# New places for the buffers of a convolution's backward pass, and two reordered steps, in a training kernel of four layers

## The chip, the cores and the metric

The kernel runs on one core of a Trainium2 chip. The metric is the time of one execution on the device, in microseconds (us). The trace is one execution recorded by the hardware profiler. Its engines are PE (TensorE, matrix products into PSUM), ACT (ScalarE), DVE (VectorE), POOL (GpSimd) and SP (SyncE, which here only issues transfers). Each engine takes its own instructions in the order in which the program was laid out, and waits for the others through semaphores.

## The reference

The program is the forward and the backward pass of four residual layers on a sequence of 2048 positions and 512 channels: convolution layer A, MLP layer B, A again, B again, with shared weights.

```python
def _A_ref(q, k, v, shift_k, ssm_k, ssm_D):          # convolution layer
    k_shift = sum over t of 4 taps: k_pad[:, t:t+S, :] * shift_k[:, ks-1-t]
    kv = k_shift * v
    y = irfft(rfft(kv padded to 2S) * rfft(ssm_k padded to 2S))[:S]
    y = y + kv * ssm_D
    return q * y

def _B_ref(x, w1, b1, w2, b2):                       # MLP, hidden width 1376
    h = gelu(einsum("bsd,df->bsf", x, w1) + b1)
    return einsum("bsf,fd->bsd", h, w2) + b2

x = A_q
x = x + _A_ref(layernorm(x), A_k, A_v, A_shift_k, A_ssm_k, A_ssm_D)
x = x + _B_ref(layernorm(x), B_w1, B_b1, B_w2, B_b2)
x = x + _A_ref(layernorm(x), ...)                    # same weights again
x = x + _B_ref(layernorm(x), ...)
# outputs: x, and by jax.vjp the gradients of q, k, v, shift_k, ssm_k, ssm_D, w1, b1, w2, b2
```

The kernel does the transforms as products with sine and cosine tables. The convolution `y` is computed once, since it doesn't depend on `x`.

## The kernel before: the parts that matter here

The run has these stages: tables and convolution forward (0 to about 210 us), MLP forward (to about 460), MLP backward (to about 640), then the backward pass of the convolution. Beside this last stage a second stream of work runs, the gradients of the MLP weights (`weight_grads`): the convolution's code yields after each step a number of microseconds, and that much of `weight_grads` is put in behind it. PE and DVE keep this program order.

**The start.** `sin_of` fills a table: phases on POOL for the first 1024 columns and on DVE for the rest, a bit mask on DVE, the sine on ACT. The constants of the fifth, five-row table `sp5` (for one tap row of the filter) are made before the first table.

```python
def sin_of(nc, consts, pool, out, krow, pv, shift, np_=P):
    for c0 in range(0, n, 1024):
        u = pool.tile([P, 1024], I32, name="tab_u", tag="tab_u", bufs=3)[0:np_, 0:w]
        eng = nc.gpsimd if c0 == 0 else nc.vector
        eng.tensor_scalar(out=u, in0=krow[...], scalar1=pv, scalar2=float(shift), ...)     # L182
    for c0, w, u in reversed(us):
        nc.vector.tensor_single_scalar(out=u, in_=u, scalar=8191, op=ALU.bitwise_and)
        nc.scalar.activation(out=out[...], in_=u, func=ACT.Sin, ...)
# phase_conv_forward
    pvh = iota_f32(...); pvn = iota_f32(...)
    pi5 = gp.tile([5, 1], I32, name="pi5")
    nc.vector.memset(pi5, 0)
    nc.gpsimd.iota(pi5[0:4, :], ...)                      # L467
    pv5 = gp.tile([5, 1], F32, name="pv5")
    nc.vector.tensor_copy(out=pv5, in_=pi5)
    ...                                                   # (cut)
    for cc in range(ND):                                  # four tables, each followed by
        sin_of(nc, consts, gp, tabN[...], krow, pvn[...], ...)
        h_chunk(cc)                                       # transposes of the filter: PE, then DVE casts hA, hsp
```

**MLP forward.** `o_ps` sums the residual and eleven products of the hidden layer in one PSUM bank.

```python
    for t in range(TS):                                   # b_fwd, TS = 4
        ps = m.psum.tile([P, D], F32, name="o_ps", tag="oo", bufs=4)
        nc.tensor.matmul(ps, lhsT=m.ident, rhs=x[:, t, :], start=True, stop=False)         # L1097
        for c in range(NFC):                              # NFC = 11
            nc.tensor.matmul(ps, lhsT=h[:, c, ...], rhs=w.w2[:, c, :], start=False, stop=(c == NFC - 1))   # L1099
        nc.scalar.activation(out=x[:, t, :], in_=ps, func=ACT.Identity)
```

**Convolution backward.** All pools here lie on the right side of SBUF; a pool that closes gives its room to the next one opened, and a new tile waits for the last use of the tiles under it (`reuse_waits="tile"`).

```python
    with tc.tile_pool(name="cb_w", side="right", ...) as wp:
        W = [wp.tile([P, 2, 8, 512], BF16, name=f"Wb{m}") for m in range(2)]
        ...                                                      # (cut) spectra, inverse blocks (DVE) into W[.][.., 4:8]
        with tc.tile_pool(name="cb_io", side="right", ...) as io:
            wdiag = io.tile([P, ND, 4, P], BF16, name="wdiag_b")
            ksbs = [io.tile([P, 4, D], BF16, name="ksb_b", tag="ksb", bufs=4) for i in range(4)]
            ...
            gT = io.tile([P, ND, S + 16], BF16, name="gksT")
            for i in range(4):
                for h in range(4):
                    gkv = W[h % 2][:, h // 2, 4 + i, :]
                    ...                                          # DVE products, PE transposes gt_ps
                    if h >= 2:
                        pr = psum.tile([P, 2, 512], F32, name="gr_ps", tag="sp", bufs=2)
                        ...                                      # 4 PE transposes
                        for cc in range(ND):                     # 4 evictions into W[1]
                            nc.scalar.activation(out=W[1][:, cc // 2, ...], in_=pr[:, 0, ...], func=ACT.Identity)   # L794
                    nc.scalar.activation(out=gT[...], in_=ps[...], func=ACT.Identity)                 # L797
                yield 3.0
                ...                                              # stores of ksb, unflip_rows
            kcs = [gyp.tile([P, 4096], BF16, name="kTc", tag="Sg", bufs=2)[:, 0:4 * 544] for cc in range(2)]
            kcs += [w0f[:, 2048 + 2176 * x:2048 + 2176 * (x + 1)] for x in range(2)]   # w0f: W[0], flat
            for cc in range(ND):
                dma(out=kcs[cc], in_=dram.kT[:, cc, :, :])       # dma = nc.gpsimd.dma_start, L809
            ...                                                  # gradient of k: 256 products gk_ps, 16 evictions, 4 stores
            gwo = io.tile([P, 2, ND, 4], F32, name="gwo", tag="gwo", bufs=1)
            junk = W[0][:, 0, 0:2, :]
            for cc in range(ND):                                 # gradient of the four taps
                for j in range(4):
                    for half in range(2):                        # g_ from gT, or from W[1]
                        nc.vector.scalar_tensor_tensor(out=junk, in0=g_, in1=kc[...], accum_out=gwo[...], ...)
                    yield 2.2
    with tc.tile_pool(name="cb_gh", side="right", ...) as hp:    # gradient of the long filter
        tabG = hp.tile([P, 2, 16, NQP], BF16, name="tabG")       # NQP = 272
        ...                                                      # 2 loads of tabG
        w0 = hp.tile([P, 2, 8, NQP], BF16, name="Wh", tag="Wh", bufs=2)
        th0 = [hp.tile([P, 2, 2, NQP], BF16, name=f"ibh{x}", tag=f"ibh{x}", bufs=3) for x in range(3)]
        gh0 = hp.tile([P, S], BF16, name="gh", tag="gh", bufs=4)
        for cc in range(ND):
            ...                      # 57 products gh_ps (PE) in 8 PSUM tiles, 11 evictions into Wh (ACT, L871 and L875)
            yield 7.0
            ...                      # inverse blocks of Wh on DVE, store of gh
```

**The weight gradients.** A unit is one chunk of 128 hidden rows of one layer: it is loaded (`dw_fm`), transposed on PE in two halves (`dw_tp`), evicted (`dw_tm`) and multiplied (16 products `dw_ps`). For the last 22 units DVE also sums `dw_fm` along its rows.

```python
    def fetch(k, sync):        # the buffer of unit k is that of unit k - 4
        fms[k] = pool.tile([P, S], BF16, name="dw_fm", tag=f"dw_fm{k % 4}", bufs=1)
        sync.dma_start(out=fms[k], in_=...)
    def sum_rows(k):
        nc.vector.tensor_reduce(out=b1a[...], in_=fms[k], op=ALU.add, ...)
    for k, (which, i, c) in enumerate(units):                    # 44 units
        fetch(k + 4, nc.sync)
        for t in range(NT):                                      # NT = 16
            if t in (2, 9): turn_half(k + 1, int(t == 9))        # 8 dw_tp, one eviction
            if t == 5: turn_out()                                # dw_pt
            if t == 12: flush(); sum_rows(k + 1)
            nc.tensor.matmul(ps, lhsT=tm[:, t, :], rhs=m.G[i][:, t, :], ...)               # dw_ps
```

Of the kernel before, what the change touches and what calls it, by code (L numbers as in the profile page):

```python
# [11 lines left out]
ACT = mybir.ActivationFunctionType  # L12
ALU = mybir.AluOpType
BF16 = mybir.dt.bfloat16
F32 = mybir.dt.float32
I32 = mybir.dt.int32
P = 128
# [392 lines left out]
def phase_conv_forward(ctx, nc, tc, dims, consts, dram, res, aps):  # L410
# [53 lines left out]
    pvn = iota_f32(nc, gp, [P, 2], [[2 * P, 2]], 0, 2, "pvn")  # L464
    pi5 = gp.tile([5, 1], I32, name="pi5")
    nc.vector.memset(pi5, 0)
    nc.gpsimd.iota(pi5[0:4, :], pattern=[[0, 1]], base=512, channel_multiplier=1024)  # L467
    pv5 = gp.tile([5, 1], F32, name="pv5")
    nc.vector.tensor_copy(out=pv5, in_=pi5)
    tabN = gp.tile([P, 2, 2, 2048], BF16, name="tabN")  # L470
# [63 lines left out]
    for m in range(2):  # L534
        for i in range(4):
            ps = psum.tile([P, 512], F32, name="hr_ps", tag="ks", bufs=2)
            nc.tensor.matmul(ps, lhsT=consts.anti, rhs=hR[:, i, m * 512:(m + 1) * 512], start=True, stop=True)
            nc.scalar.activation(out=hB[:, i, m * 512:(m + 1) * 512], in_=ps, func=ACT.Identity)
    for gi, (k1, base, n) in enumerate(GROUPS):
        for f in range(2):  # L540
            sin_of(nc, consts, gp, sp5[:, gi, f, :], krow[0:5, base * P:(base + 1) * P], pv5, 2048 * (1 - f), np_=5)
# [166 lines left out]
def conv_backward(ctx, nc, tc, dims, consts, dram, res, aps):  # L708
# [27 lines left out]
    with tc.tile_pool(name="cb_w", bufs=1, side="right", reuse_waits="tile") as wp:  # L736
# [18 lines left out]
        for m in range(2):  # L755
# [6 lines left out]
            yield 16.0  # L762
        with tc.tile_pool(name="cb_io", bufs=1, side="right", reuse_waits="tile") as io:
            wdiag = io.tile([P, ND, 4, P], BF16, name="wdiag_b")
            dma(out=wdiag, in_=dram.wdiag)
            ksbs = [io.tile([P, 4, D], BF16, name="ksb_b", tag="ksb", bufs=4) for i in range(4)]
            vbs = []
            for i in range(4):
# [4 lines left out]
                tok_io(nc, vbs[i], v_ap, dram.vB, i, eng=nc.gpsimd)  # L773
            gT = io.tile([P, ND, S + 16], BF16, name="gksT")
            nc.vector.memset(gT[:, :, S:S + 16], 0.0)
            for i in range(4):
                vb, ksb = vbs[i], ksbs[i]
                for h in range(4):
# [8 lines left out]
                    if h >= 2:  # L787
                        pr = psum.tile([P, 2, 512], F32, name="gr_ps", tag="sp", bufs=2)
                        for cc in range(ND):
                            cs = slice(cc * P, (cc + 1) * P)  # L790
                            nc.tensor.matmul(pr[:, 0, cs], lhsT=gkv[:, cs], rhs=consts.ident, start=True, stop=True)
                        for cc in range(ND):
                            c0 = 256 * (i % 2) + P * (h - 2)
                            nc.scalar.activation(out=W[1][:, cc // 2, 2 * (cc % 2) + i // 2, c0:c0 + P],  # L794
                                                 in_=pr[:, 0, cc * P:(cc + 1) * P], func=ACT.Identity)
                    t0 = 512 * i + (P * h if h < 2 else 512 - P * (h - 1))
# [4 lines left out]
                if i % 2:  # L801
                    with tc.issue_after(last.ins):
                        unflip_rows(nc, aps[f"out_{i // 2}"].flatten_outer_dims(), (dram.o0B, dram.o1B)[i // 2],
                                    eng=nc.gpsimd)
            w0f = W[0][:, :, :, :].rearrange("p e s d -> p (e s d)")
            kcs = [gyp.tile([P, 4096], BF16, name="kTc", tag="Sg", bufs=2)[:, 0:4 * 544] for cc in range(2)]
            kcs += [w0f[:, 2048 + 2176 * x:2048 + 2176 * (x + 1)] for x in range(2)]
            for cc in range(ND):
                dma(out=kcs[cc], in_=dram.kT[:, cc, :, :].rearrange("p i w -> p (i w)"))  # L809
            unflip_rows(nc, out3, dram.o3B, eng=nc.gpsimd)  # L810
            for t in range(NT):
# [8 lines left out]
                if t % 4 == 3:  # L820
                    dma(out=out2[(t - 3) * P:(t + 1) * P, :].rearrange("(t p) d -> p t d", p=P), in_=go)
            gwo = io.tile([P, 2, ND, 4], F32, name="gwo", tag="gwo", bufs=1)
            junk = W[0][:, 0, 0:2, :].rearrange("p a (b d) -> p (a b) d", b=2)
            for cc in range(ND):
                kc = kcs[cc].rearrange("p (i w) -> p i w", i=4)
                for j in range(4):
                    for half in range(2):
                        if half == 0:
                            g_, k_ = gT[:, cc, 0:S].rearrange("p (i q) -> p i q", i=4)[:, :, 0:256], 16 - j
                        else:  # L830
                            g_ = W[1][:, cc // 2, 2 * (cc % 2):2 * (cc % 2) + 2, :].rearrange("p a (b q) -> p (a b) q", b=2)
                            k_ = 272 + j
# [6 lines left out]
    with tc.tile_pool(name="cb_gh", bufs=1, side="right", reuse_waits="tile") as hp:  # L839
        NQ = 257  # L840
        NQP = 272
        tabG = hp.tile([P, 2, 16, NQP], BF16, name="tabG")
        for f in range(2):
            dma(out=tabG[:, f, :, 0:256], in_=dram.tabG[:, f])
        last = nc.gpsimd.tensor_copy(out=tabG[:, :, :, 256], in_=consts.col256)
        with tc.issue_after(last.ins):
            dma(out=out4.rearrange("(c p) j -> p c j", p=P), in_=gwb)
        w0 = hp.tile([P, 2, 8, NQP], BF16, name="Wh", tag="Wh", bufs=2)
        th0 = [hp.tile([P, 2, 2, NQP], BF16, name=f"ibh{x}", tag=f"ibh{x}", bufs=3) for x in range(3)]
        gh0 = hp.tile([P, S], BF16, name="gh", tag="gh", bufs=4)  # L850
        gdo = hp.tile([P, ND], BF16, name="gdo")
# [223 lines left out]
def b_fwd(nc, m, x, l, s):  # L1075
# [19 lines left out]
    for t in range(TS):  # L1095
        ps = m.psum.tile([P, D], F32, name="o_ps", tag="oo", bufs=4)
        nc.tensor.matmul(ps, lhsT=m.ident, rhs=x[:, t, :], start=True, stop=False)  # L1097
        for c in range(NFC):
            nc.tensor.matmul(ps, lhsT=h[:, c, t * P:(t + 1) * P], rhs=w.w2[:, c, :], start=False,  # L1099
                             stop=(c == NFC - 1))  # L1100
        nc.scalar.activation(out=x[:, t, :], in_=ps, func=ACT.Identity)
        yield 2.5
# [339 lines left out]
```

## Time and profile before

| what | value |
|---|---|
| time, median of 3 | 955.77 us (954.72 to 958.27) |
| span of the profiled execution | 952.4 us, mean TensorE clock 0.944 of full speed |
| PE busy | 794.6 us, 83% |
| DVE busy | 734.0 us, 77% |
| ACT busy | 613.5 us, 64% |
| POOL busy | 151.7 us, 16% |
| bytes moved by transfers | 180.87 MB, mean 190 GB/s |

The shares are means over stages with different limits: a stage is read from its own stretch of the trace, by what each engine waited for there. In the lists below a line gives start, duration, engine, line of the kernel, operation, output and inputs. A number in brackets is the engine's idle time just before, and what ended it. Line L55 is a helper that keeps PE and DVE instructions in program order, so most of those have this one line and are told apart by tile names. "Wb" is `W`; "Wh" the tile `w`/`w0` of the last stage; "b1a" the row sums.

### The profile page before, as it was taken

To read this page: it belongs to the slowest core of one execution; us is meant where nothing else is said; L and a number is where in the kernel's file an instruction comes from. 1 tells how busy PE (TensorE), PEld (TensorE's weight loads), DVE (VectorE), ACT (ScalarE), POOL (GpSimd) and SP (SyncE) were. 2 spreads that over 40 slices of the span, in tenths; PEclk is the share of its full clock that TensorE was granted. 3 is DMA by queue.
4 is the path that set the end of the run, shared out by engine and by line. 5 is a ranking of instruction groups with operands and counts; after the bars stand their busy time and mean duration, and the time that the engine had idled before them with its cause. 6 is when DMAs were issued, how large, how long until landed. Compare 5 with 4: busy or idle time off the path is not lost.

```text
span 952.4 us, 12919 instructions
## 1 busy us (share of the span) xinstructions
PE 794.6 (83%) x4754; PEld 406.6 (43%) x4754; DVE 734.0 (77%) x1203; ACT 613.5 (64%) x810; POOL 151.7 (16%) x274
## 2 busy tenths in 40 slices
PE   3698868846786869649999999968999997995998
PEld 2463324422332324214444444434455555853664
DVE  7748489895999979658458878883389995699973
ACT  5867645637997979579835656445665558652664
POOL 5632210021001010100001221220011304200000
PEclk9999999978998789869999999979999999997999
DMA  6568786223445344476798868549076798852331
GB/s 218 173 237 322 280 286 222 90 50 105 138 150 146 130 140 148 139 215 180 249 283 241 246 190 239 166 151 353 2 244 203 266 323 287 288 170 72 118 100 38
DMA packets 157079, 180.87 MB, mean 190 GB/s; under 512 B 50325, under 2 KB 137048, under 8 KB 156504
## 3 DMA queue, kind: packets, MB, share of 16 engines
q1 hardware_dynamic: 142872, 135.70, 46.1%
q0 software_dynamic: 11968, 40.15, 11.7%
q10 hardware_dynamic: 2176, 4.19, 1.2%
q8 instruction: 37, 0.61, 0.3%
q14 instruction: 26, 0.21, 0.1%
HBM read 95.76 MB, written 82.13 MB: 187 GB/s over the span
## 4 chain that ended last, share of the span: by engine, by line
PE 37%; DVE 30%; ACT 17%; DMA 6%; issue 6%; POOL 3%; SPq 1%; ACTq 0%; DVEq 0%; POOLq 0%
PE gn_ps L1134 7%; PE sp_ps L55 7%; PE gh_ps L1116 6%; DVE Wb L55 6%; PE dw_ps L55 6%; ACT g_z L1089 3%; PE gh_ps L55 3%; DVE b1a L55 3%; ACT g_s L1065 3%; ACT g_o L1066 2%; ACT g_q L1062 2%; DVE pr_t L55 2%; DVE pr_u L55 2%; PE z_ps L1087 2%; DMA tabFb<-tabF_d 2%
## 5 line engine op out<-in xcount | busy, mean ns | idle before, releaser
L55 PE MATMUL dw_ps<-G,dw_tm 128*128 128x512 bf16 x704 | 170.8, 381 | 2.2 <-ACT dw_tm L1236 2.2
L1236 ACT ACTIVATE dw_tm<-dw_tp 128x1024 bf16<-128x1024 bf16 x88 | 89.9, 1024 | 68.2 <-PE dw_tp L55 68.2
L1087 PE MATMUL z_ps<-nT_sl,w_sb 128*128 128x512 bf16 x352 | 93.8, 424 | 32.3 <-DMA nT_sl<-n_sl 27.2
L1099 PE MATMUL o_ps<-w_sb,h_sl 128*128 128x512 bf16 x352 | 92.1, 404 | 26.7 <-DVE h_sl L1069 26.4
L55 PEld LDWEIGHTS <-dw_tm 128*128 128x128 bf16 x704 | 64.9, 98 | 62.5 <-ACT dw_tm L1236 2.9
L1118 ACT ACTIVATE gz_sl<-gh_ps 128x512 bf16<-128x512 f32 x88 | 50.2, 594 | 56.5 <-PE gh_ps L1116 53.3
L1134 PE MATMUL gn_ps<-w1T_sb,gz_sl 128*128 128x512 bf16 x352 | 81.4, 379 | 1.3 <-DVE gz_sl L1119 1.3
L1116 PE MATMUL gh_ps<-gT_sl,w2T_sb 128*128 128x512 bf16 x352 | 79.6, 379 | 0.0
L1087 PEld LDWEIGHTS <-w_sb 128*128 128x128 bf16 x352 | 37.3, 107 | 88.4 <-issue 43.0
L1089 ACT ACTIVATE g_z<-z_ps,b1col 128x512 bf16<-128x512 f32 x88 | 55.2, 708 | 27.6 <-PE z_ps L1087 27.6
L1099 PEld LDWEIGHTS <-h_sl 128*128 128x128 bf16 x352 | 35.1, 103 | 79.0 <-DVE h_sl L1069 35.3
L55 PEld LDWEIGHTS <-dw_fm 128*128 128x128 bf16 x704 | 47.8, 100 | 20.9 <-issue 0.8
L55 PE MATMUL dw_tp<-ident,dw_fm 128*128 128x128 bf16 x704 | 54.8, 222 | 0.0
L1134 PEld LDWEIGHTS <-gz_sl 128*128 128x128 bf16 x352 | 34.3, 98 | 43.2 <-DVE gz_sl L1119 2.3
L1116 PEld LDWEIGHTS <-w2T_sb 128*128 128x128 bf16 x352 | 34.4, 98 | 41.1
L55 DVE TENSOR_REDUCE b1a<-dw_fm 128x1 f32<-128x2048 bf16 x22 | 49.6, 2277 | 0.0
L989 POOL TENSOR_SCALAR rstd<-ln_mv 128x4 f32<-128x4 f32 x16 | 7.6, 475 | 248.1 <-DVE ln_mv L987 161.9
L1146 POOL TENSOR_SCALAR bb_diag<-ident,bb_cols 128x128 bf16<-128x128 bf16 x32 | 21.6, 676 | 157.3 <-DVE bb_junk L1143 148.1
L1065 ACT ACTIVATE g_s<-g_t 128x2048 bf16<-128x2048 bf16 (+1 forms) x24 | 42.8, 1784 | 3.6 <-DVE g_t L1064 3.6
L1119 DVE TENSOR_TENSOR gz_sl<-gz_sl,gpb 128x2048 bf16<-128x2048 bf16 (+1 forms) x24 | 27.2, 1134 | 22.7 <-DMA gpb<-gp_d 11.7
L1062 ACT ACTIVATE g_q<-g_z 128x2048 bf16<-128x2048 bf16 (+1 forms) x24 | 43.1, 1798 | 0.1
L1066 ACT ACTIVATE g_o<-g_t 128x2048 bf16<-128x2048 bf16 (+1 forms) x24 | 42.7, 1780 | 0.0
(297 smaller groups left out, 1621.6 us busy)
## 6 DMA issues: line engine op xcount, KB each, us to landing
dw_fm<-h_d SPq DMA_DIRECT2D x22, 512.0 KB, 3.9
dw_fm<-gz_d SPq DMA_DIRECT2D x22, 512.0 KB, 3.8
h_d<-h_sl SPq DMA_DIRECT2D x16, 512.0 KB, 2.9
gp_d<-g_p SPq DMA_DIRECT2D x16, 512.0 KB, 3.3
nb_sl<-n_d SPq DMA_DIRECT2D x16, 512.0 KB, 5.3
gpb<-gp_d SPq DMA_DIRECT2D x16, 512.0 KB, 4.5
gz_d<-gz_sl SPq DMA_DIRECT2D x16, 512.0 KB, 5.2
n_d<-n_sl SPq DMA_DIRECT2D x12, 512.0 KB, 3.3
```

What stands on the lines that cost most here:

```text
L55: return self.tc.keep_in_program_order(f(*args, **kwargs))
L1062: nc.scalar.activation(out=q, in_=zb, func=ACT.Square)
L1065: nc.scalar.activation(out=sg, in_=t, func=ACT.Sigmoid)
L1066: nc.scalar.activation(out=o, in_=t, func=ACT.Sigmoid, scale=-1.0)
L1087: nc.tensor.matmul(ps, lhsT=w.w1[:, dc, c * P:(c + 1) * P], rhs=nT[:, dc, :], start=(dc == 0), stop=(dc == ND - 1))
L1089: nc.scalar.activation(out=zb[:, c - c0, :], in_=ps, func=ACT.Identity, bias=w.b1col[:, c:c + 1])
L1099: nc.tensor.matmul(ps, lhsT=h[:, c, t * P:(t + 1) * P], rhs=w.w2[:, c, :], start=False, stop=(c == NFC - 1))
L1116: nc.tensor.matmul(ps, lhsT=w.w2T[:, dc, c * P:(c + 1) * P], rhs=gT[:, dc, :], start=(dc == 0), stop=(dc == ND - 1))
L1118: nc.scalar.activation(out=gz[:, c, :], in_=ps, func=ACT.Identity)
L1119: nc.vector.tensor_tensor(out=gz[:, c0:c0 + k, :], in0=gz[:, c0:c0 + k, :], in1=gp[:, 0:k, :], op=ALU.mult)
L1134: nc.tensor.matmul(ps, lhsT=gz[:, c, t * P:(t + 1) * P], rhs=w.w1T[:, c, :], start=(c == 0), stop=(c == NFC - 1))
L1236: nc.scalar.activation(out=dst, in_=ps, func=ACT.Identity)
```

## The change

It has three parts.

1. **Buffers of the convolution's backward pass.** The operands of the tap gradient leave `W`: the turned halves go to `gr` and the third piece of k to `kcs[2]`, both in `gy_bf` (free once the inverse blocks are done), the fourth piece to a tile of its own, `kc3`, and the throw-away output `junk` also to `gy_bf`. `gr` is laid out so that one eviction takes the place of four. In `cb_io` the tiles `gT`, `gwo` and `kc3` come first, and in `cb_gh` the tiles `gh`, `ibh` and `Wh` come ahead of `tabG`. The aim is that the tiles of the last stage which are filled first lie on room that is free early, and not under operands of the tap gradient.
2. **MLP forward.** The residual joins `o_ps` as the last product of its group, not the first.
3. **The start.** The phases of the five-row table are made after the four big tables.

```diff
-    pi5 = gp.tile([5, 1], I32, name="pi5")
-    nc.vector.memset(pi5, 0)
-    nc.gpsimd.iota(pi5[0:4, :], pattern=[[0, 1]], base=512, channel_multiplier=1024)
-    pv5 = gp.tile([5, 1], F32, name="pv5")
-    nc.vector.tensor_copy(out=pv5, in_=pi5)
... (the same five lines now stand behind the tables and the products hr_ps)
+            gT = io.tile([P, ND, S + 16], BF16, name="gksT")
+            gwo = io.tile([P, 2, ND, 4], F32, name="gwo")
+            kc3 = io.tile([P, 4 * 544], BF16, name="kTc3")
             wdiag = io.tile([P, ND, 4, P], BF16, name="wdiag_b")
...
-            gT = io.tile([P, ND, S + 16], BF16, name="gksT")
+            tf = res.gy_bf[:, :, :].rearrange("p t d -> p (t d)")
+            gr = tf[:, 0:4096].rearrange("p (c i q) -> p c i q", c=ND, i=4)
...
-                        for cc in range(ND):
-                            c0 = 256 * (i % 2) + P * (h - 2)
-                            nc.scalar.activation(out=W[1][:, cc // 2, 2 * (cc % 2) + i // 2, c0:c0 + P],
-                                                 in_=pr[:, 0, cc * P:(cc + 1) * P], func=ACT.Identity)
+                        nc.scalar.activation(out=gr[:, :, i, P * (h - 2):P * (h - 1)],
+                                             in_=pr[:, 0, :].rearrange("p (c t) -> p c t", c=ND), func=ACT.Identity)
...
-            kcs += [w0f[:, 2048 + 2176 * x:2048 + 2176 * (x + 1)] for x in range(2)]
+            kcs += [tf[:, 4096:4096 + 2176], kc3]
...
-            gwo = io.tile([P, 2, ND, 4], F32, name="gwo", tag="gwo", bufs=1)
-            junk = W[0][:, 0, 0:2, :].rearrange("p a (b d) -> p (a b) d", b=2)
+            junk = tf[:, 6272:6272 + 1024].rearrange("p (i q) -> p i q", i=4)
...
-                            g_ = W[1][:, cc // 2, 2 * (cc % 2):2 * (cc % 2) + 2, :].rearrange("p a (b q) -> p (a b) q", b=2)
+                            g_ = gr[:, cc]
...
+        gh0 = hp.tile([P, S], BF16, name="gh", tag="gh", bufs=4)
+        th0 = [hp.tile([P, 2, 2, NQP], BF16, name=f"ibh{x}", tag=f"ibh{x}", bufs=3) for x in range(3)]
+        w0 = hp.tile([P, 2, 8, NQP], BF16, name="Wh", tag="Wh", bufs=2)
         tabG = hp.tile([P, 2, 16, NQP], BF16, name="tabG")
... (the same three lines are gone from behind the loads of tabG)
-        nc.tensor.matmul(ps, lhsT=m.ident, rhs=x[:, t, :], start=True, stop=False)
         for c in range(NFC):
-            nc.tensor.matmul(ps, lhsT=h[:, c, t * P:(t + 1) * P], rhs=w.w2[:, c, :], start=False,
-                             stop=(c == NFC - 1))
+            nc.tensor.matmul(ps, lhsT=h[:, c, t * P:(t + 1) * P], rhs=w.w2[:, c, :], start=(c == 0), stop=False)
+        nc.tensor.matmul(ps, lhsT=m.ident, rhs=x[:, t, :], start=False, stop=True)
```

## Prediction

> **What bounds the kernel now.** I read the page's busy shares first, then busy times by stage, then the chain of work that ended last with its timeline in the stage that the change touches most, and last the waits at the start and in the MLP forward. Busy time by stage (core, stretch, its length, busy us with count of PE, PEld, DVE, ACT, POOL; granted clock, DMA share, GB/s):
>
> ```profile
> 782.00:812.00 30.00, 24.76 (x232) 15.93 (x231) 16.66 (x36) 23.69 (x60) 12.97 (x15) 1.00 0.87 301
> 812.00:861.00 49.00, 49.00 (x519) 34.31 (x517) 42.12 (x53) 29.89 (x40) 5.70 (x7) 1.00 0.69 210
> 861.00:873.00 12.00, 0.25 (x2) 0.10 (x1) 11.69 (x18) 0.80 (x2) 0.00 (x0) 0.61 0.26 77
> 873.00:952.40 79.40, 74.27 (x568) 48.98 (x566) 55.92 (x84) 44.86 (x74) 3.70 (x6) 0.97 0.28 83
> ```
>
> PE is full from 812 to 861, stands still for twelve microseconds while DVE works, and is nearly full to the end. The timeline of that stage, cut to what matters:
>
> ```profile
> 818.08 1.22 DVE L55 SCALAR_TENSOR_TENSOR Wb<-gksT,kTc 128x1024 bf16<-128x1024 bf16 x1 [18.88 <-DMA kTc<-kT_d]
> ...
> 870.88 1.22 DVE L55 SCALAR_TENSOR_TENSOR Wb<-gksT,Wb 128x1024 bf16<-128x1024 bf16 x1
> ...
> 872.20 1.09 ACT L871 ACTIVATE Wh<-gh_ps 128x514 bf16<-128x514 f32 x2 [11.40 <-DVE Wb L55]
> 872.85 7.65 PE L55 MATMUL gh_ps<-tabG,GY 128*128 128x257 bf16 x48 [11.75 <-ACT Wh L871]
> ...
> 888.49 5.51 PE L55 MATMUL gh_ps<-tabG,GY 128*128 128x257 bf16 x48 [0.25 <-ACT Wh L871]
> ```
>
> PE has filled both PSUM tiles of `gh_ps`; ACT may not empty them into `Wh` until the last product that reads `gksT` is over on DVE. That is no data dependence: `Wh` lies on `gksT`'s room. The start, by the same view:
>
> ```profile
> 9.05 1.12 POOL L182 TENSOR_SCALAR tab_u<-krow,pvn 128x1024 int32<-128x1024 f32 x1
> ...
> 10.25 0.12 POOL L467 IOTA pi<- 4x1 int32 x1
> 10.36 1.11 POOL L182 TENSOR_SCALAR tab_u<-krow,pvn 128x1024 int32<-128x1024 f32 x1
> 10.40 0.14 DVE L55 CAST pv<-pi 5x1 f32<-5x1 int32 x1 [3.85 <-POOL pi L467]
> 10.47 1.54 DVE L55 TENSOR_SCALAR tab_u<-krow,pvn 128x1024 int32<-128x1024 f32 x1
> ```
>
> DVE waits 3.85 us for a five-row constant that is needed 20 us later. Of the waits in the MLP forward (us in total, times, longest) one concerns the change; there ACT is the fullest engine (205 of 245 us from 215 to 460, PE 184):
>
> ```profile
> PE o_ps L1099 <- DVE h_sl L1069: 26.4, 10, 10.3
> ```
>
> [...]
>
> **The buffers: the wait at 861.** Sizes in bytes per partition from the tile shapes, counted from the top T of the pools; that a pool starts at its lower end is my reading of "right side", tested below. Before, `cb_w` is T-32768 to T (two `W` of 16384). `cb_io` under it holds wdiag 4096, four ksb of 4096, gT 16512, gwo 128: ksb is T-65792 to T-49408, gT T-49408 to T-32896. `cb_gh` comes to 70816: tabG 17408 from T-70816, then two Wh of 8704 from T-53408. So tabG lies on wdiag and ksb, and the first Wh on the last ksb and on gT. Both fit the trace: tabG's load is issued at 832.88, after the last store of `gk_o` (tag ksb, issued 827.21), and Wh is let go when gT's last reader ends. After, gT, gwo and kc3 (4352) stand at the bottom of `cb_io` (T-74240 to T-53248), wdiag to T-49152, ksb to T-32768; `cb_gh` has gh (16384) from T-70816, nine ibh (19584) from T-54432, Wh from T-34848, tabG from T-17440. The first Wh lies on the last ksb and the first `W`; tabG on the end of the first `W` and on the second. Since the tap gradient leaves `W`, that room is free after the transposes (about 808) and the `gk_o` stores (about 833): well before 860. What still lies under gT and kc3 (gh, ibh) is written by DVE itself, behind its own reads.
>
> PE began the group at 859.95. A group without the wait takes 887.09 to 894.00, 6.91 us, and so would end at 866.9, not at 880.50: **13.6 us**, of which 11.75 are the wait and nearly 2 the slow clock.
>
> **Does PE keep these 13.6 us?** It must not run into DVE, which stays in the tap gradient until 873.3: 32 products of 1.27 us with their readout, and row sums of 2.28 us between. What PE needs from DVE later: a `dw_fm` load reuses the buffer of the fourth unit before, after its row sum. I moved each PE time after 880 by -13.6. Unit 35 is then turned at 870.2; its load follows the row sum that ends at 858.7. Unit 36: 881.5 against 865.9. Unit 37: 885.9 against 875.6. With 4 to 8 us to landing this last one has 2 to 6 us to spare, and all later ones over 10. Filter chunk 2 needs the first Wh back from DVE at about 887.7; DVE's inverse blocks end at 886.9 before, and 1.2 us sooner when ACT's evictions are long done. Chunk 3 has 2 to 3 us. DVE's last row sum was over at 936.3; its five waits for Wh after 875 (1.17, 1.10, 1.08, 1.29, 2.15) add to 6.8 us and fall away, so it ends near 929.5, before PE at 947.45 - 13.6 = 933.9. So PE stays the bound and the gain reaches the end. The 18.88 us for which DVE waits on k then cost nothing, but only 2 us of delay there are free.
>
> **One eviction for four.** Eight times, four ACT operations in 0.78 us give way to one of about 0.60 (as gksT's, 0.598). PE waits for this eviction four times for 0.29 us: perhaps **0.7 us**.
>
> **The start.** Without the cast DVE starts its phases at 6.55, not 10.47. Its mask of the other half still needs POOL's phases, ready at 10.17, where it has to get in before POOL's next instruction. The first casts of hA then start at about 10.9 instead of 13.26: 2.4 us; 1.3 us if POOL's next 1.11 us goes first. I take **2.0 us**. From there to 60 us the chain runs through DVE, ACT and PE without a transfer, so it should be kept. The constant's new place costs nothing: its users wait for ACT's evictions of hB, which end at 32.31.
>
> **The residual.** Count and cost of the products are equal (379 ns each). As first product it ran while PE waited for h; as last it comes after. In each of ten waits four groups may be open, so 1 to 4 products at 0.22 us apart move behind it: up to 0.9 us each, where ACT isn't the limit anyway. On the other side the residual no longer takes a PSUM bank before any h is ready (two at 201, then 10.79 us of waiting for a third). ACT's order there has its own wait for POOL until 220.87, so I see no gain at the start. I take **0.8 us of loss**, within three either way, as the order of ACT and PE may be laid out anew.
>
> **Sum.** -13.6 - 0.7 - 2.0 + 0.8 = -15.5, from 955.8: **940.3 us**.
>
> **Rivals.** (1) DVE becomes the bound of the last stage: it is full from 818 to 873 and 13 us behind PE in the program already. PE would stop for `dw_fm` of unit 37 or for Wh of chunk 2. For it: loads of 8.2 us median between 780 and 875, and the moved k pieces and tabG may get into the queue ahead of the piece that DVE awaits. Every microsecond beyond 2 comes off the gain; with 6 the time is 944. (2) k comes earlier, since two of its pieces no longer wait for `W` and can be loaded before the stores crowd the queue: DVE starts before 818, but PE is full there, so nothing more than 1 us: 939. (3) The new Wh finds another late reader under it, say a store of ksb: the wait moves and only the start remains: 953. The sizes speak against it. (4) The MLP forward is laid out better or worse by up to 4 us: 936 to 944.
>
> **Range and chances.** (1) and (4) are the likely errors, both of a few microseconds: 935 to 948 for 8 in 10. The 2% line is 936.7, 3.6 us under my number; I give 0.24 to being under it. Slower by 2% would need a new wait of over 30 us: 0.02. The rest, 0.74, lies within.
>
> **What would show it.** Right: no PE wait before `gh_ps` near 858; its 48 products in about 5.5 us; ACT's Wh not released by the tap gradient; PE without gaps to the end; hA's first cast near 11. Wrong: PE turns waiting for `dw_fm` or `gh_ps` for Wh between 870 and 900 (rival 1), Wh released by a transfer (rival 3), or a stage from 215 to 460 that is longer by more than a microsecond.

## The result

| kernel | time, median (range, runs) | ratio to the kernel before, 95% interval |
|---|---|---|
| before | 955.44 us (954.72 to 958.27, 4) | 1 |
| changed | 941.40 us (940.25 to 944.56, 4) | 0.9853 (0.9822 to 0.9884) |

940.3 us were predicted, with 935 to 948 as the range. The profiled execution of the changed kernel is the slowest of its four (944.56 us, span 942.8), so the two profiles differ by 9.6 us where the medians differ by 14.0; where the other 4 us arise is part of what follows.

Busy time by stage in the changed kernel, in the columns of the table of before, with the stages bounded where the same steps stand now (transposes of the gradient, gradient of k, the old place of the wait, the rest):

```profile
785.41:814.92 29.51, 24.81 (x224) 15.76 (x227) 17.39 (x36) 22.71 (x36) 10.26 (x12) 1.00 0.91 314
814.92:863.35 48.43, 48.11 (x512) 33.92 (x516) 40.56 (x51) 29.30 (x40) 7.36 (x8) 1.00 0.63 197
863.35:876.00 12.65, 12.35 (x103) 8.98 (x103) 12.40 (x19) 8.78 (x16) 0.00 (x0) 1.00 0.31 93
876.00:942.80 66.80, 60.66 (x471) 39.90 (x475) 56.38 (x84) 37.60 (x60) 3.70 (x6) 0.99 0.34 99
```

The third row is the answer to the row of before in which PE did 0.25 us of work in 12. It now does 12.35 in 12.65, at full clock, and DVE does 12.40 us of the tap gradient and the row sums beside it. The timeline of the same stretch:

```profile
822.16 1.23 DVE L55 SCALAR_TENSOR_TENSOR gy_bf<-gksT,kTc 128x1024 bf16<-128x1024 bf16 x1 [18.81 <-DMA kTc<-kT_d]
...
863.68 0.82 PE L55 MATMUL gh_ps<-tabG,GY 128*128 128x257 bf16 x6
864.10 1.09 ACT L871 ACTIVATE Wh<-gh_ps 128x514 bf16<-128x514 f32 x2
864.76 5.50 PE L55 MATMUL gh_ps<-tabG,GY 128*128 128x257 bf16 x48 [0.25 <-ACT Wh L871]
...
874.76 1.23 DVE L55 SCALAR_TENSOR_TENSOR gy_bf<-gksT,kTc 128x1024 bf16<-128x1024 bf16 x1
```

ACT's first eviction into `Wh` has no wait behind it, and starts at 864.10, while DVE reads `gksT` for the last time at 874.76: the tie is cut. The 48 products take 5.50 us, not 7.65. DVE still waits 18.81 us for its piece of k, as before (18.88), and it does not matter. The start:

```profile
6.07 3.79 POOL L601 TENSOR_SCALAR col<-col,alt 128x2 bf16<-128x2 bf16 x10
6.59 0.75 DVE L55 TENSOR_SCALAR tab_u<-krow,pvn 128x1024 int32<-128x1024 f32 x1
7.37 0.69 DVE L55 TENSOR_SCALAR tab_u<-tab_u 128x1024 int32<-128x1024 int32 x1
10.11 2.83 POOL L182 TENSOR_SCALAR tab_u<-krow,pvn 128x1024 int32<-128x1024 f32 x2
11.26 0.69 DVE L55 TENSOR_SCALAR tab_u<-tab_u 128x1024 int32<-128x1024 int32 x1 [3.19 <-POOL tab_u L182]
11.87 1.28 DVE L55 CAST hA<-ha_ps 128x512 bf16<-128x512 f32 x2
```

DVE begins its phases at 6.59 us, as predicted, but then waits 3.19 us for POOL, whose own phases start at 10.11 and not at 9.05. `hA` comes 1.39 us earlier (13.26 to 11.87). Last, the waits that concern `o_ps` in the MLP forward (215 to 465 us; total, times, longest):

```profile
PE o_ps L1098 <- DVE h_sl L1069: 27.2, 10, 10.3
...
ACT x_sl L1100 <- PE o_ps L1099: 1.4, 5, 0.3
```

The second is new: five times ACT waits 0.27 us for the residual's product, which is now the last of its group.

To see where time went I divided each timeline at steps that all kernels have: the first transpose of the gradient (`gt_ps`), the first product of the gradient of k (`gk_ps`), the first product of the long filter's gradient (`gh_ps<-tabG`) and a transpose near the end (`b_ps`). Between the first and the last of these the lengths of the same stretch hardly differ from execution to execution, and the changes stand out:

| stretch (us) | before | phases alone | residual alone | changed | changed, again | buffers alone |
|---|---|---|---|---|---|---|
| first gt_ps to first gk_ps | 25.13 | 25.13 | 25.14 | 24.39 | 24.38 | 24.38 |
| first gk_ps to first gh_ps<-tabG | 48.44 | 48.44 | 48.43 | 48.43 | 48.43 | 48.44 |
| first gh_ps<-tabG to last b_ps | 87.50 | 89.20 | 87.80 | 73.86 | 73.86 | 73.86 |

Ahead of 786 us this is not so: the first `gt_ps` starts anywhere between 786.2 and 790.9 us, in changed and unchanged kernels alike. That spread is the 4 us above (786.38 before, 790.53 changed). About half of them arise ahead of the first `g_z`, the first step of the MLP forward on ACT (221.59 before, 223.57 changed), and the experiments found their place. The other half lie between it and `gt_ps` (564.79 us before, 566.96 changed). That long stretch takes 563.3 to 568.8 us in the fourteen profiles of this document, and what sets its length stays open.

### The profile page after: what moved, and what is told of

The parts are those of the page before. It is cut to its first block, busy times and chain, and to the rows that moved or that the text cites. A ratio compares the mean times of both kernels' runs of the same rounds, so it can differ in the third digit from the quotient of the medians.

```text
span 942.8 us, 12817 instructions
## 1 busy us (share of the span) xinstructions
PE 792.6 (84%) x4674; PEld 407.7 (43%) x4754; DVE 732.8 (78%) x1203; ACT 613.0 (65%) x786; POOL 154.6 (16%) x274
## 4 chain that ended last, share of the span: by engine, by line
PE 51%; ACT 18%; DVE 15%; issue 6%; DMA 6%; POOL 3%; SPq 1%; ACTq 0%; POOLq 0%; DVEq 0%
PE dw_ps L55 14%; PE gn_ps L1133 7%; PE gh_ps L1115 7%; PE sp_ps L55 6%; PE iv_ps L55 4%; PE dw_tp L55 4%; ACT g_z L1089 3%; PE gh_ps L55 3%; ACT g_s L1065 3%; ACT g_q L1062 2%; PE z_ps L1087 2%; ACT g_o L1066 2%; DMA tabFb<-tabF_d 2%; DMA nT_sl<-n_sl 2%; ACT n_sl L1009 2%
## 5 line engine op out<-in xcount | busy, mean ns | idle before, releaser
L55 PE MATMUL dw_ps<-G,dw_tm 128*128 128x512 bf16 x673 | 167.2, 383 | 4.3 <-ACT dw_tm L1235 2.5
L1098 PE MATMUL o_ps<-w_sb,h_sl 128*128 128x512 bf16 x344 | 89.5, 398 | 30.2 <-DVE h_sl L1069 27.2
L1069 DVE TENSOR_TENSOR h_sl<-g_s,g_z 128x2048 bf16<-128x2048 bf16 (+1 forms) x24 | 27.1, 1129 | 20.2 <-ACT g_s L1065 20.2
```

The costliest lines, as they stand in the source:

```text
L55: return self.tc.keep_in_program_order(f(*args, **kwargs))
L1069: nc.vector.tensor_tensor(out=h, in0=sg, in1=zb, op=ALU.mult)
```

## The experiments

Differences in microseconds are the ratio to the kernel before, measured on the same chip in the same series, times its 956 us.

### The changed kernel again

Nothing was edited.

> The changed kernel once more, unaltered, for the spread of its time and of its profile. In its first profile everything from 84 to 811 us stood 2.0 to 4.2 us later than in the kernel before, although the start had gained 1.4 us; in that stretch a cold clock at 80 to 84 us is seen. Theory A (that loss is luck of one profile, whose run at 944.6 us was the slowest of four): the first g_z then starts near 220 rather than 223.6, the first gh_ps near 860 to 861 rather than 863.35, and the time is 940 to 942 us. Theory B (the loss belongs to the change, above all to the residual's new place): the same steps stand again at 223 to 224 and at 863, and the time is 943 to 945 us. In both the 48 products of gh_ps take about 5.5 us and start without a wait.

Measured: 944.19 us (941.83 to 948.58), ratio 0.9873 (0.9846 to 0.9901), so 12.1 us less than before (9.5 to 14.7). In its profile the first `g_z` starts at 219.37 and the first `gh_ps` of the last stage at 859.39, each 4 us earlier than in the first profile of the same kernel. Theory A holds for the profile: the delay of the first profile is not the change's. The time is B's figure rather than A's, but the kernel before is at 956.75 us in this series, 1.3 us over the first, and single executions of one kernel lie 7 us apart. So the ratio is what counts, and the two ratios agree within their intervals.

### One part at a time

Buffers alone (the kernel before, with part 1 of the change):

> The kernel before with part 1 alone (new places of the buffers, one eviction for four). Theory (the removed wait of PE at 861 is nearly all of the gain): 13.6 us less than the kernel before, 0.7 more from the single evictions, so about 941.3 us, and the start and the MLP forward as before. Rival (the parts depend on each other, or the rest of the change pays for part of it): more than 943.5 us, or under 939 us.

Residual alone (part 2):

> The kernel before with part 2 alone (the residual as the last product of its group). Theory of the prediction: 0.8 us slower, with an uncertainty of 3 either way. Rival (the residual's product as first kept PE from the next group's z_ps while it waited, and is worth something as last): 1 to 3 us faster. Second rival (what the first profile of the change showed, 1.9 to 2.6 us more at the end of the MLP forward and 1.6 us more in the MLP backward, comes from this part): 2 to 4 us slower. In each case the wait of PE at 861 is still there, about 11.7 us.

Constant of the five-row table alone (part 3):

> The kernel before with part 3 alone (the five-row constant made behind the tables). Theory: hA's first cast starts at 11.9 rather than 13.26 us, 1.4 us earlier, since DVE's earlier start slows POOL's own operations (their time 2.7 to 3.8 us); about 1 us of it is still there at 80 us and at the end, so 954.4 us. Rival of the prediction: 2.0 us, 953.4 us. Second rival (the start's gain is lost on the way, in waits with a slack or in the clock): no difference, 955.4 us.

| kernel | median | ratio (95%) | difference |
|---|---|---|---|
| buffers alone | 944.07 us | 0.9862 (0.9838 to 0.9885) | -13.2 us (-15.5 to -11.0) |
| residual alone | 957.78 us | 1.0017 (1.0001 to 1.0033) | +1.6 us (+0.1 to +3.2) |
| constant alone | 956.74 us | 0.9998 (0.9981 to 1.0015) | -0.2 us (-1.8 to +1.4) |

The buffers are the whole gain: -13.2, with -11.8 as the sum of the three, beside -14.0 and -12.1 for the change in its two series. By the number alone its 944.07 us would be the rival's (over 943.5), but the kernel before is slower in this series too; as a difference the theory's -14.3 lies inside the interval. The residual costs a little. The constant gives nothing that these times can show, although its profile has the gain where it arises: `hA` at 11.90, and the first `tt_ps` (the transposes of a table) at 74.33 instead of 75.42. It is lost between there and 165 us (below).

What the residual does is seen at the end of the forward pass. From DVE's last `h_sl` to PE's next task it is 2.65 us with the residual first (460.10 to 462.75, buffers alone) and 3.52 with it last (460.41 to 463.93, residual alone): 0.87 us, four products of 0.22. Whether it costs anything at the other waits of the forward pass is not shown.

### The old order of the last stage's tiles

```diff
 (cb_gh of the changed kernel; operands of the tap gradient stay out of W)
-        gh0, th0, w0, then tabG
+        tabG, then w0, th0, gh0
```

> The changed kernel with one thing undone: tabG, Wh, ibh and gh stand in their old order (tabG lowest). The operands of the tap gradient stay out of W. Theory (which tile lies on which room decides): tabG then lies on the room of gksT and kTc3, which DVE reads until about 877 us, so its load is issued only then and takes about 8 us; PE has no products gh_ps to do before about 885 and loses some 20 us: 960 to 966 us, slower than the kernel before. Rival (it is enough that the tap gradient's operands have left W): 941 to 945 us as the changed kernel.

Measured: 973.74 us (973.40 to 974.05), ratio 1.0183 (1.0167 to 1.0198): 17.5 us slower than the kernel before. PE and POOL in its timeline:

```profile
861.56 0.59 PE L55 MATMUL dw_ps<-G,dw_tm 128*128 128x512 bf16 x2
886.82 0.61 PE L55 MATMUL gh_ps<-tabG,GY 128*128 128x257 bf16 x2 [24.67 <-DMA tabG<-tabG_d]
...
890.43 8.85 PE L55 MATMUL gh_ps<-tabG,GY 128*128 128x257 bf16 x54 [2.78 <-DMA tabG<-tabG_d]
```

```profile
879.16 2.31 POOL L844 DMA_DIRECT2D tabG<-tabG_d  x2 [49.47 <-DVE gwb L55]
```

The direction and the cause are the theory's: `tabG` lies on `gksT`, `gwo` and `kTc3`, so its load is held back for 49.47 us until DVE is through with the tap gradient. The reader that the trace names is the last of the three: `gwb`, which DVE makes from `gwo` at 878.06, one row sum behind the last product (874.71). The size was 10 us short. From the step before the wait to the end of the program it is 109.45 us here (862.15 to 971.6) against 79.45 in the changed kernel (863.35 to 942.8): 30 us more. The table lands in two halves, so there are two waits, 24.67 and 2.78; and the products after them are slow, 54 in 8.85 us where at 5.50 for 48 they would take 6.19, another 2.7. These three make 30.1. Taking the operands out of `W` is thus not enough: without the new order of the tiles the change would have made the kernel slower than it was.

### Four evictions again

```diff
-    activation(out=gr[:, :, i, P*(h-2):P*(h-1)], in_=pr[:, 0, :].rearrange("p (c t) -> p c t", c=ND), ...)
+    for cc in range(ND):
+        activation(out=gr[:, cc, i, P*(h-2):P*(h-1)], in_=pr[:, 0, cc*P:(cc+1)*P], ...)
```

> The changed kernel with four evictions into gr again instead of one. Theory: four waits of PE on ACT of 0.29 us each come back near 790 us, and the first gk_ps comes 0.7 to 0.8 us later after the transposes begin; time 0.7 us more than the changed kernel, which is less than these times spread, so the trace decides. Rival (ACT has slack there and the four waits were not on the path): the stretch from the first gt_ps to the first gk_ps is as long as in the changed kernel.

Measured: 942.45 us, ratio 0.9864 (0.9842 to 0.9885), not to be told from the changed kernel. The waits of PE from 780 to 814 us have the old line again, which the changed kernel lacks:

```profile
PE gr_ps L55 <- ACT gy_bf L797: 1.2, 4, 0.3
```

The stretch to the first `gk_ps` is 26.82 us, 2.44 more than 24.38. Of that 1.7 is something else: at 796.00 nine `dw_ps` products take 3.69 us, where nine take 2.11 elsewhere, and the eight `dw_tp` behind them 0.75 instead of 0.61, at a granted clock of 0.57 from 796 to 800 us, a slow spell that the changed kernel's profiles don't have there (1.00 from 785 to 814 us in both). The rest, 0.72, fits the 0.75 us between 25.13 and 24.38 in the table of stretches, where three profiles have four evictions and three have one.

### Does DVE bound the last stage?

Two runs change only when DVE is done with the tap gradient. First earlier:

```diff
-            for cc in range(ND):              # the tap gradient's loop
+            for cc in (3, 2, 0, 1):           # pieces of k that land early come first
```

> The changed kernel with the tap gradient's channel blocks taken in the order 3, 2, 0, 1, so that the two pieces of k that are loaded early (issued at 760 and 778 us) are used first. Theory (PE is the bound of the last stage, DVE's wait of some 19 us for k is slack): that wait is gone or under 5 us, DVE is in the tap gradient earlier and through it several us earlier, and the time stays within 1 us of the changed kernel. Rival (DVE bounds the last stage): 3 to 8 us faster.

Then later, by six products done twice:

```diff
                         nc.vector.scalar_tensor_tensor(out=junk, in0=g_, ..., accum_out=gwo[:, half, cc, j:j + 1])
+                        if cc == 3 and j:
+                            nc.vector.scalar_tensor_tensor(...)          # the same once more
```

> The changed kernel with six products of the tap gradient done twice on DVE (extra work, 6 times 1.27 us, the same results), so that DVE leaves the tap gradient 7.6 us later, near 884 us. It measures the slack of the prediction's first rival. Theory of the prediction: DVE may be late by 2 us at filter chunk 2, 2 to 3 at chunk 3 and 2 to 6 at the load of unit 37, so 7.6 us of delay cost 2 to 5.5 us, seen as waits of PE for Wh or dw_fm after 885: 945 to 949 us. Rival (DVE has far more slack than was worked out): less than 1 us, PE without a gap. Second rival (DVE is the bound): all of 7.6 us, 950 us or more.

Earlier: 941.97 us, ratio 0.9847 (0.9832 to 0.9861). DVE's wait for k is gone:

```profile
808.00 1.23 DVE L55 SCALAR_TENSOR_TENSOR gy_bf<-gksT,kTc 128x1024 bf16<-128x1024 bf16 x1 [6.59 <-ACT gksT L799]
...
862.67 1.22 DVE L55 SCALAR_TENSOR_TENSOR gy_bf<-gy_bf,kTc 128x1024 bf16<-128x1024 bf16 x1
```

Its first product starts at 808.00 rather than 822.16 and its last at 862.67 rather than 876.03, eleven microseconds earlier when counted from each profile's first `gh_ps` (861.02 and 863.35); the stretch from there to the last `b_ps` is 73.86 us in both. PE is the bound, and the wait for k was slack.

Later: 950.55 us, ratio 0.9944 (0.9925 to 0.9962), so 5.4 us under the kernel before and, by the two ratios of the changed kernel, 7 to 9 over it. By its length that could be the second rival, in which all of the 7.6 us come through. The timeline says otherwise. All that PE waits for between 885 and 895 us:

```profile
887.37 0.62 PE L55 MATMUL dw_tp<-ident,dw_fm 128*128 128x128 bf16 x8 [1.56 <-DMA dw_fm<-gz_d]
...
894.48 8.28 PE L55 MATMUL gh_ps<-tabG,GY 128*128 128x257 bf16 x48 [4.86 <-ACT Wh L875]
```

These are the two places that the prediction's first rival named. The turn of unit 37 was put at 885.9 (it begins its wait at 885.81), the first `Wh` of chunk 2 at 887.7 (it begins at 888.06 when the first wait is taken off). PE stops for 1.56 + 4.86 - 0.25 = 6.2 us, so the slack was 1.4 of the 7.6 us; 2 were predicted. At unit 37 it was 7.6 - 1.56 = 6.0 us, of 2 to 6 predicted. The expected loss was too small all the same, since it left out the slow products behind a stop: the 48 after the wait take 8.28 us, not 5.50. The stretch is 82.96 us, 9.1 longer for 7.6 us of delay. In the changed kernel DVE is not the bound, but it is within two microseconds of being one.

### Does the wait at 861 slow the clock?

```diff
 (the kernel before, ahead of the group of products that waits)
+    for x in range(52):
+        nc.tensor.matmul(warm, lhsT=consts.ident, rhs=Y[:, 0, 0, :], start=True, stop=True)   # read by nobody
```

> The kernel before with 52 needless products (512 wide, read by nobody) put on PE in front of the group that waits at 861 us, so that PE stays busy while it waits. Theory (the slow clock after the wait is a cost of its own): the 48 products gh_ps after the wait take about 5.5 us instead of 7.65, and the stretch from the first gh_ps to the last b_ps is 85.0 to 85.7 us instead of 87.5 to 89.2; of it 11.8 us are the wait's own. Rival (the products are slow for another reason, such as ACT's readout): still about 7.6 us.

```profile
863.08 11.39 PE L55 MATMUL warm_ps<-GY,ident 128*128 128x512 bf16 x51
874.85 5.51 PE L55 MATMUL gh_ps<-tabG,GY 128*128 128x257 bf16 x48 [0.39 <-ACT Wh L876]
```

The group takes 5.51 us, and the stretch from the first `gh_ps` to the last `b_ps` 85.21 us: 2.3 to 4.0 less than in the three profiles with an idle wait (87.50, 87.80, 89.20). In the profile the slow products after this wait (7.65 us in the kernel before, at a granted clock of 0.71 from 872.85 to 880.50) are a cost of their own. The time shows less than that: 954.87 us, ratio 0.9993 (0.9979 to 1.0006), -0.7 us (-2.0 to +0.6). A profile is one execution; why the timed ones gain less than the stretch stays open.

### Where the start's gain goes

```diff
+    kT_store = nc.gpsimd.dma_start(out=dram.kT, in_=kT)
-    for k1, base, n in GROUPS:                     # fill of the constant table col (POOL)
+    with tc.issue_after(kT_store.ins):             # ... behind the big tables
```

> The changed kernel with the fill of a constant table (twenty operations, used only after 200 us) put behind the big tables on POOL, so that POOL's phases start at about 6.6 rather than 10.1 us. hA's first cast should start near 9 us, 3 us earlier than in the changed kernel and 4 us earlier than before. Theory A (what is gained at the start is kept): 2 to 3 us faster than the changed kernel. Theory B (what is gained at the start is lost again before 215 us, as with the phases alone, which gave 1.4 us at hA and nothing in the time): the time is within 1 us of the changed kernel, and the first g_z doesn't start earlier than the spread of the profiles so far (219.4 to 224.2 us).

Measured: 944.30 us, ratio 0.9874 (0.9856 to 0.9892): nothing beside the changed kernel, though the start did what was expected:

```profile
6.67 3.62 POOL L182 TENSOR_SCALAR tab_u<-krow,pvn 128x1024 int32<-128x1024 f32 x2 [0.53 <-DVE pvn L55]
...
9.31 1.27 DVE L55 CAST hA<-ha_ps 128x512 bf16<-128x512 f32 x2
```

Theory B, then: the first `g_z` starts at 220.22. But where is it lost? The early stages divided in the same way (`hA` is DVE's first cast, `tt_ps` the first transpose of a table, `KVg` the last eviction of a spectrum) show one stretch that varies by 4.5 us. The one ahead of it, from `hA` to `tt_ps`, varies by 1.3 (61.2 to 62.4 us), and the one behind it up to the first `g_z` by 0.04:

| kernel | hA | first tt_ps to last KVg | clock in it | last KVg to first g_z |
|---|---|---|---|---|
| before | 13.26 | 89.70 | 0.98 | 56.47 |
| buffers alone | 13.28 | 90.12 | 0.94 | 56.50 |
| residual alone | 13.28 | 92.13 | 0.93 | 56.48 |
| constant alone | 11.90 | 93.37 | 0.91 | 56.49 |
| changed | 11.87 | 92.83 | 0.91 | 56.46 |
| changed, again | 11.89 | 88.89 | 0.96 | 56.48 |
| constant table's fill late | 9.31 | 92.84 | 0.91 | 56.48 |

PE has the same work in it each time, and the stretch is, roughly, the longer the lower the clock. On average it takes back the whole gain of the constant: of all runs here, the four profiles with `hA` at 13.3 us have the first `g_z` at 222.2 (221.6 to 223.0), and the seven with `hA` at 11.9 have it at 222.2 too (219.4 to 224.2). What differs is what PE does after a short wait. The changed kernel in its first profile:

```profile
78.16 1.93 PE L55 MATMUL tt_ps<-ident,tabN 128*128 128x128 bf16 x16 [2.82 <-ACT tg L200]
...
82.26 1.89 PE L55 MATMUL sp_ps<-fold_d,tabN 128*128 128x512 bf16 x4
```

and the same kernel in its second:

```profile
77.89 0.61 PE L55 MATMUL tt_ps<-ident,tabN 128*128 128x128 bf16 x8 [2.82 <-ACT tg L200]
...
80.52 1.04 PE L55 MATMUL sp_ps<-fold_d,tabN 128*128 128x512 bf16 x4
```

The wait is 2.82 us in both, and after it four products take 1.89 us in one and 1.04 in the other. That is half speed against full, and the granted clock says the same: from 77.5 to 84 us it is 0.50 in the first profile and 1.00 in the second. The kernel before too is at 0.50 after this wait, but only from 79 to 82 us. One program, one wait, two outcomes: what decides between them is not shown.

The test: keep PE busy there.

```diff
+    def keep_warm(n):
+        ps = psum.tile([P, D], F32, name="warm_ps", tag="ks", bufs=2)
+        for _ in range(n):
+            nc.tensor.matmul(ps, lhsT=consts.ident, rhs=tabF[:, 0, 0, 0:512], start=True, stop=True)
...
+    keep_warm(11)                     # ahead of the third tt_ps
+    keep_warm((8, 14, 5)[g - 1])      # ahead of the first three groups of iv_ps
```

> The changed kernel with the constant table's fill behind the big tables, as in the run before with that edit, and besides 38 needless products (512 wide, into a free PSUM tile) on PE in four waits between 70 and 150 us: 11 before the third tt_ps, 8, 14 and 5 before the first three groups of iv_ps. So far, in ten profiles, the stretch from the first tt_ps to the last KVg took 88.9 to 93.4 us, the longer the lower the granted clock in it (0.96 to 0.98: 88.9 to 89.7; 0.91: 92.8 to 93.4), while the stretch after it up to the first g_z is 56.5 us in all ten. Theory (what the start gained is eaten there by the slow clock after short waits): with PE busy the clock stays at 0.97 or more, the stretch takes 88.5 to 89.5 us, the first g_z starts near 216.5 us and the time is about 3 us under that of the run without the products, 940 to 941 us. Rival (the stretch is set by DVE, ACT or transfers, the clock only goes along): the stretch takes 91 to 93 us whatever the clock, no gain.

The whole stretch, the run without these products and the run with them (columns as in the table by stage):

```profile
70.90:163.74 92.84, 77.50 (x390) 33.32 (x390) 71.30 (x127) 53.57 (x57) 12.94 (x25) 0.91 0.76 270
```

```profile
72.17:161.28 89.11, 78.50 (x420) 34.47 (x428) 71.34 (x127) 52.97 (x57) 12.92 (x25) 1.00 0.78 280
```

With more work on PE the stretch is 3.7 us shorter, at a clock of 1.00, and the first `g_z` starts at 217.73. That is 3.9 us ahead of the kernel before (221.59), as `hA` is (9.31 against 13.26): all of the start's gain is still there. The time is 938.84 us, ratio 0.9820 (0.9798 to 0.9843), against 0.9874 without: 5 us less (2.4 to 7.9, from the two intervals), and a little under the 940 to 941 that were named. The 3 expected lie within, and the profile bears out only 2.5 us at the first `g_z` (220.22 to 217.73). At the first `gt_ps` it is 8.0 us (788.99 to 780.99), but the other 5.5 come from the long stretch behind `g_z`, which has the same work in both kernels; the two are its longest and its shortest. The rival is out: the early stretch follows the clock (92.84 us at 0.91, 89.11 at 1.00). So a gain at the start was not lost to another engine; it was paid out again on the way, in slow products. Why the loss comes out about as large as the gain over many executions, and not now larger and now smaller, isn't explained by this and stays open.

### All that helped, together

```diff
 (the changed kernel with the fill late, the needless products and the order 3, 2, 0, 1, and)
+        nc.tensor.matmul(ps, lhsT=m.ident, rhs=x[:, t, :], start=True, stop=False)      # residual first again
```

> The new places of the buffers and the late five-row constant, with the residual as first product again, the constant table's fill late, the needless products in the early waits, and the tap gradient's blocks in the order 3, 2, 0, 1. If the residual's new place costs 1 to 2 us, as the run with it alone says, and the products keep the start's gain, this is 938 to 940 us, the fastest. If the residual's place costs nothing: as the run with the products, 940 to 941 us.

Measured: 935.50 us (934.95 to 937.66), ratio 0.9792 (0.9771 to 0.9814): 19.9 us faster than the kernel before (17.8 to 21.9), and faster than the changed one, 2.5 us under what was expected. Its stretch from `tt_ps` to `KVg` takes 89.00 us at a clock of 1.00, its last stretch 73.86 us. Between this and the run with the needless products stand two edits, the residual's place and the order of k; the order alone gave nothing in the bounded stage, so the 2.7 us between the ratios fit the residual's 1.6 (0.1 to 3.2). The two edits were not taken apart, though, and the intervals of the two ratios overlap.

## Why the prediction was right, point by point

- **The wait at 861: -13.6 predicted.** 13.64 in the pair of profiles that it was worked out on (87.50 - 73.86), 13.9 and 15.3 with the other two profiles that have the wait, and -13.2 (-15.5 to -11.0) in the times, with the single evictions. The layout reckoned from the tile sizes held: the run with `tabG` at the bottom waits for the last reader of the three tiles that the sizes put under it. That pools on the right side start at their lower end, which was a reading and no measurement, is borne out by it. The split into a wait and a slow clock held in the profile (7.65 us for the 48 products at a granted clock of 0.71, 5.51 with PE kept busy); in the times of that run the slow clock's share does not show (-0.7 us, -2.0 to +0.6).
- **PE keeps it: right.** The slack of 2 us at filter chunk 2 came out as 1.4, and PE stopped at the two places named when DVE was made late. What the rival lacked was the slow products behind a stop (8.28 us for 48 that take 5.50 elsewhere): this one cost 2.8 us beyond its own length.
- **One eviction for four: -0.7 predicted, -0.75 measured** in the stretch of the profiles (25.13 to 24.38); the times can't show so little.
- **The start: -2.0 predicted; this term failed.** It failed twice. The step "its mask of the other half still needs POOL's phases, ready at 10.17" took POOL's times as fixed. With DVE at work from 6.59 us POOL's ten small operations take 3.79 us instead of 2.74, its phases come at 11.2, and 1.4 us are left. With the fill moved away POOL's two phase operations take 3.62 us beside DVE, where one took 1.12 while DVE waited. That DVE's mask has to get in before POOL's next operation was the author's estimate, and no run shows it: in the kernel before DVE's phases took 1.54 us at 10.47 beside POOL's, and 0.73 at 14.66 ahead of them, but in the changed one the mask took 0.69 us at 11.26 beside POOL's second phase operation, and it was POOL's that was longer, 1.62 us. The alternative of 1.3 us that the prediction set beside it had the size right and another reason. Then "from there to 60 us the chain runs through DVE, ACT and PE without a transfer, so it should be kept": it was kept to 74 us (1.1 in that pair; 1.2 between the means of the four and the seven profiles above), and then the next stretch took it back (92.83 us at a granted clock of 0.91, 89.70 at 0.98 in the kernel before). In the times -0.2 us (-1.8 to +1.4).
- **The residual: +0.8 within three; +1.6 (0.1 to 3.2) measured.** The mechanism, up to 0.9 us behind the last `h`, is seen with 0.87. The sign and the size were right within what can be measured.
- **Sum.** -15.5 predicted, -14.0 and -12.1 in the two series, -11.8 from the parts. Of the 3.7 us between the prediction and the parts, the start is 1.8, the buffers 1.1 and the residual 0.8; the last two lie within their intervals. Of the rivals, (2) k earlier and (3) another late reader did not come about; (1) stood 1.4 us off; (4) is the residual. Whether k is held up by the stores ahead of it in POOL's queue was not tested: in the kernel before a store issued at 800.64 took 15.9 us to land, and the two pieces of k issued from 802.30 on took 16.1 (median).

## What to carry to other kernels

When a wait ends at an engine whose data the waiting one doesn't use, work out which tile lies on which, to the byte, for both layouts: moving operands away and moving the tile that is filled first are two halves, and the first without the second made this kernel 17.5 us slower (the second without the first was not tried). Before a short gain far ahead of the end is counted, look for waits of PE behind it (four of 2.12 to 3.51 us in the kernel before), and for the clock after them (0.50 after the one of 2.82): filling them with products that nobody reads gave 2.5 us in the profile here, and 5 (2.4 to 7.9) in the times. And when a wait has been removed, count the slack of the next engine; here it was 1.4 us, and taking the tap gradient's blocks in another order let DVE through eleven microseconds earlier.

## What the runs showed of the hardware

- A wait of PE of 2.82 us was followed by half speed in some executions and by full speed in others of the same kernel (four products 512 wide in 1.89 or 1.04 us, at a granted clock of 0.50 or 1.00). Of the twelve profiles with that wait, eight have the sixteen transposes right behind it at half speed (1.92 or 1.93 us). The stretch with this and three more waits (2.12, 3.51 and 2.38 us in the kernel before) took 88.9 to 93.4 us, and with PE kept busy in them 89.0 and 89.1 us in two profiles.
- Two stops of PE in the last stage cost 2.1 and 2.8 us beyond their length in the profiles: 48 products took 7.65 us after 11.75 us of waiting (granted clock 0.71), 8.28 after 4.86, and 5.50 after 0.25.
- Beside DVE's integer phases at 6.59 us POOL's ten small operations took 3.79 us, and 2.74 where DVE waited.
- In one profile nine products took 3.69 us instead of 2.11 at 796 us, in a place where the waits of PE ahead of them (1.15 us the longest) are those of the other profiles. The cause is open.
